# Forty-eight one-row reads from the Pool queue beside a saturated load stream

## The chip, the cores and the metric

The kernel runs on one core of one Trainium2 chip. The metric is device microseconds of one execution. The time before is the median of three runs.

## The reference

Two independent problems, A and B, have the same shapes, and their outputs stand side by side. Each is one step of decoding with attention over a window of a cache, for two batch entries, 32 query heads and 16 key/value heads of width 128. Cut to what matters:

```python
def ref(x, k_cache, v_cache, wq, wo):          # x [2, 1, 576], caches [2, 16, 16384, 128]
    W = 4096                                    # only the last 4096 positions are used
    q = (x @ wq).reshape(B, 1, 32, 128).transpose(0, 2, 1, 3)
    k = repeat(k_cache[:, :, Sk - W:, :], 2, axis=1)
    v = repeat(v_cache[:, :, Sk - W:, :], 2, axis=1)
    p = softmax(einsum("bhqd,bhkd->bhqk", q, k) * 128 ** -0.5)
    o = einsum("bhqk,bhkd->bhqd", p, v)
    return o.transpose(0, 2, 1, 3).reshape(B, 1, 4096) @ wo   # wo [4096, 576]
out = concatenate([ref(A), ref(B)], axis=-1)    # [2, 1, 1152], bfloat16
```

All tensors are bfloat16. The windows of the keys and values, with the two pairs of weights, make 153 MB that have to be read from HBM once.

## The kernel before

The work is cut into 16 slabs (`NSLAB`). A slab is one problem, one group of four key/value heads and one batch entry: its keys are one transfer of 4096 KB (called K), its values another (called V). Two slabs with the same heads and the two batch entries form a group G, and there are eight groups. A ring of four slots in SBUF (`ring`, `NSLOT = 4`) holds K and V transfers in turn.

All of these loads, and those of the weights `wq` and `wo`, are issued from SP's queue in one fixed order: K of slab t, then V of slab t - 3, with a `wo` piece (M or W) after every second group. SP issues a load when the slot's last reader is done: the second transpose of a K slab on DVE, or the last product with a V slab on PE.

One turn of the main loop (`for t in range(NSLAB)`, L664) does, for slab t: two transposes of K on DVE, one for each half (`make_X`, L433, into `xt`), each followed by the score products on PE (`make_S`, L459 and, through the helper, L264, into `st`); the products need a mask of queries, `zq`, which Pool builds two slabs ahead (`make_Z`, L425). For the group before, it takes the maximum on DVE (`make_max`, L467), reduces it on Pool (`mv` and `m`, L469 and L470), turns `m` on PE (L473), takes the negative maximum on DVE (`nM`, L480), repeats it on Pool (`nMrep`, L483), and forms the bias of the exponentials (L487 on PE, L490 on DVE, L497 on ACT). The probabilities are transposed on DVE (`pT`, L506), and the value products of slab t - 3 run on PE (L536), scaled and reduced on DVE (L559, L566).

Each engine runs its instructions in the order in which the program adds them; between engines there are semaphores. The order on Pool in an odd turn t is: `rsum` of a group, then `zq` of slab t + 2. In the even turn after it: `mv` and `m` of the group just finished, `zq`, `nMrep`. A `zq` waits until PE has finished the scores of slab t.

`sel` is a constant of 128 partitions by 4 x 128 elements, built on Pool at the start (L208). Four products on PE at the start (L307, `op_qs`) read it to spread the queries, and nothing reads it afterwards.

At the end of the program SP waits until both outputs have been written:

```python
        emit("sp", nc.sync)
        nc.sync.wait_ge(out_sem, dma_count[out_sem])
```

Before the change Pool issues no transfer. ACT's queue issues five small ones: four of two rows for `x` at the start and one output.

Of the kernel before, what the change touches and what calls it, by code (L numbers as in the profile page):

```python
# [62 lines left out]
def build_kernel(nc, probs, out):  # L63
# [4 lines left out]
    x0, k0, v0, wq0, wo0 = probs[0]  # L68
# [24 lines left out]
    with es:  # L93
# [15 lines left out]
        sel = sb("sel", [128, 4, 128], BF16)  # L109
# [44 lines left out]
        sem = lambda name: es.enter_context(nc.semaphore(name))  # L154
# [7 lines left out]
        wo_sem = [sem("wo%d" % r) for r in range(2)]  # L162
        x_sem = [sem("xload%d" % P) for P in range(NPROB)]
        out_sem = sem("outdone")

        S = _Sched()
        dma_count = {}

        def dma_op(eng, sem_h, n_dmas, fn, deps, tag):
            op = S.add(eng, fn, deps, tag)  # L170
            dma_count[sem_h] = dma_count.get(sem_h, 0) + 16 * n_dmas
            op.dma = (sem_h, dma_count[sem_h])
            return op
# [16 lines left out]
        pool = lambda fn, deps, tag: S.add("pool", fn, deps, tag)  # L190
# [61 lines left out]
        def tb_job(fn, tag, deps):  # L252
            n = tbn[0]
            tbn[0] += 1
            bank = TB
            d = list(deps)
            if n >= 1:
                d.append(tb_consumer[n - 1])
            op = pe(lambda e, bank=bank: fn(e, bank), d, tag)
            return n, bank, op  # L260
# [48 lines left out]
        n_, bank_s, op_qs = tb_job(f_qs, "qs", [qte, p_sel])  # L309
# [101 lines left out]
        def make_Z(t):  # L411
            P, g, b = t // (2 * GP), (t // 2) % GP, t % 2
            deps = [qs_ev, p_zq, d_bm]
            if t >= 2:
                deps.append(Sop[(t - 2, 1)])

            def f(e):
                for kp in range(2):
                    m = 2 * b + kp
                    b0 = zq[:, 0, m, 16 + 4 * m:16 + 4 * m + 1]  # L420
                    dst = bass.AP(b0.tensor, b0.offset, [list(b0.ap[0]), [4 * 144, 4], [32, 4], [1, 4]])
                    o = b * Hq + 8 * g + 4 * kp
                    src = qs[:, P, :].rearrange("d (p w) -> d p w", p=4)[:, :, o:o + 4].unsqueeze(2).broadcast_to([128, 4, 4, 4])
                    msk = bmask[:, 0:4].unsqueeze(1).unsqueeze(3).broadcast_to([128, 4, 4, 4])
                    last = e.tensor_tensor(dst, src, msk, ALU.mult)  # L425
                return last
            Zop[t] = pool(f, deps, "Z%d" % t)

        def make_X(t, jh):
            ensure(("K", t))  # L430
            r = slot_of[("K", t)]
            deps = [stream_dma[("K", t)][0][2], Sop[(t - 1, jh)] if t >= 1 else d_xT[1]]
            Xop[(t, jh)] = dve(lambda e: e.transpose(  # L433
                xt[:, jh, :].bitcast(FP32).rearrange("p (kp x kt) -> p x kp kt", kp=2, kt=2),
                ring[:, r, jh * HW_:(jh + 1) * HW_].bitcast(FP32).rearrange("p (x kp kt) -> p x kp kt", kp=2, kt=2)), deps, "X%d_%d" % (t, jh))
            if jh == 1:
                last_reader[("K", t)] = Xop[(t, jh)]

        def make_S(t, jh):
            G, b = t // 2, t % 2  # L440
            st = STT[G % 2]
            deps = [Xop[(t, jh)], Zop[t]]
            if b == 0 and G >= 2:
                deps.append(exp_op[G - 2])

            def f(e):
                for kp in range(2):
                    for p4 in range(4):
                        b32, par = p4 // 2, p4 % 2
                        m = 2 * b + kp  # L450
                        wt = zq[:, p4, m, 16 - 16 * jh:144 - 16 * jh]
                        first = b == 0 and jh == 0 and kp == 0 and p4 == 0
                        for bk in range(2):
                            o = 4096 * kp + 2048 * bk + 32 * b32 + par
                            b0 = xt[:, jh, o:o + 1]
                            mv_ = bass.AP(b0.tensor, b0.offset, [list(b0.ap[0]), [64, 32], [2, 16]])
                            ob = st[:, 512 * bk:512 * bk + 512]
                            if bk == 0:
                                last = e.matmul(ob, wt, mv_, start=first, stop=True, skip_group_check=True)  # L459
                            else:  # L460
                                last = mm_held(e, ob, wt, mv_, first)
                return last
            Sop[(t, jh)] = pe(f, deps, "S%d_%d" % (t, jh))

        def make_max(G):
            st = STT[G % 2]
            ch[(G, "max")] = dve(lambda e: e.tensor_reduce(mx[:], st[:, :].rearrange("p (x t) -> p t x", t=2), AX.X, ALU.max),  # L467
                                 [Sop[(2 * G + 1, 1)]] + prev(G, "pick"), "max%d" % G)
            ch[(G, "mult")] = pool(lambda e: e.tensor_tensor(mv[:], mx[:], v2[:], ALU.mult), [ch[(G, "max")], p_v2] + prev(G, "pick"), "mult%d" % G)  # L469
            ch[(G, "pick")] = pool(lambda e: e.tensor_tensor(m1[:], mv[:, 0:1], mv[:, 1:2], ALU.add), [ch[(G, "mult")]] + prev(G, "Tm"), "pick%d" % G)  # L470

        def make_Tm_pe(G):
            n, b, op = tb_job(lambda e, bank: e.transpose(bank[0:1, 0:128], m1[:, 0:1], ident_f[:]), "Tm%d" % G, [ch[(G, "pick")], p_ident_f])  # L473
            ch[(G, "Tm")] = op
            tm_job[G] = (n, b)
# [27 lines left out]
        def make_pT(G):  # L503
            v = G % 2
            deps = [exp_op[G]] + ([PVop[2 * (G - 2) + 1]] if G >= 2 else [qt_op])
            pT_op[G] = dve(lambda e: e.transpose(  # L506
                pT[:, v, :].rearrange("p (w j q) -> p j w q", w=4, q=8),
                pR[:].rearrange("p (j w q) -> p j w q", w=4, q=8)), deps, "pT%d" % G)

        def make_rsum(G):  # L510
            ch[(G, "rsum8")] = pool(lambda e: e.tensor_tensor(
                rsum8[:], rsum4[:, 0:4].unsqueeze(1).broadcast_to([128, 2, 4]), bsel[:, 0:2].unsqueeze(2).broadcast_to([128, 2, 4]), ALU.mult),
                [exp_op[G], d_bs] + prev(G, "sums"), "rsum8_%d" % G)
# [150 lines left out]
        for t in range(NSLAB):  # L664
            i = t - LAG
            odd = t % 2 == 1
            Gc = (t - 2) // 2 if not odd and t >= 2 else None
            Gs = (t - 3) // 2 if odd and t >= 3 else None
            Gd = (t - 5) // 2 if odd and t >= 5 else None
            Gp = (t - 6) // 2 if not odd and t >= 6 else None  # L670
            make_X(t, 0)
            make_S(t, 0)
            if i >= 1:
                make_evac(i - 1)
            if Gp is not None:
                make_pick(Gp)
            if Gc is not None:
                make_max(Gc)
            if Gs is not None:
                make_rsum(Gs)  # L680
                make_pT(Gs)
            if Gc is not None:
                make_Tm_pe(Gc)
            make_X(t, 1)
            make_S(t, 1)
            if t + 2 < NSLAB:
                make_Z(t + 2)
            if Gc is not None:
                make_nM(Gc)
            if Gs is not None:  # L690
                make_sums(Gs)
            if Gd is not None:
                make_dg(Gd)
            if Gp is not None and Gp % 2 == 1:
                make_projm(Gp // 2)
                if (Gp + 1) % GP == 0:
                    make_E(Gp // GP)
            if Gc is not None:
                make_bias(Gc)
            if t == T:  # L700
                make_max(NG - 1)
                make_pick(Gd)
            if i >= 0:
                make_PV(i)
# [34 lines left out]
        for e in ENGS:  # L739
            n = 0  # L740
# [13 lines left out]
        for op in order:  # L754
            have = seen[op.eng]
            need = {}
            for d in op.deps:
# [3 lines left out]
                k = id(s_h)  # L761
# [14 lines left out]
        def emit(eng_name, engine):  # L776
            for op in S.ops[eng_name]:
                for s_h, val in waits_of[id(op)]:
                    engine.wait_ge(s_h, val)
                last = op.fn(engine)  # L780
                if op.dma is None:
                    last.then_inc(ev[eng_name], 1)

        emit("sp", nc.sync)
        nc.sync.wait_ge(out_sem, dma_count[out_sem])
        emit("pe", nc.tensor)
        emit("dve", nc.vector)
        emit("act", nc.scalar)
# [35 lines left out]
```

## Time and profile before

| | before |
|---|---|
| median of 3 runs | 363.18 us (363.11 to 363.32) |
| profiled execution: span from first to last instruction | 361.8 us |
| mean granted TensorE clock | 0.849 |
| PE / DVE / ACT / POOL busy, share of the span | 66% / 60% / 13% / 7% |
| SP's queue (q1), share of 16 DMA engines' span | 98.7% |
| read from HBM | 153.10 MB, 423 GB/s over the span |

The profiled execution's time is known only as its span; the difference to the median, 1.4 us, is what lies around it. Matmuls are pipelined, so a busy PE is not PE at its peak. The share of the DMA engines is the mean over the core's 16. A packet is one piece of a transfer on one DMA engine; a completion is the packet of 4 bytes that counts up a semaphore when the pieces before it are written. In the views, a bracket behind a line gives the idle time before it and what ended it.

### The profile page before, as it was taken

To read this page: it belongs to the slowest core of one execution; us is meant where nothing else is said; L and a number is where in the kernel's file an instruction comes from. 1 tells how busy PE (TensorE), PEld (TensorE's weight loads), DVE (VectorE), ACT (ScalarE), POOL (GpSimd) and SP (SyncE) were. 2 spreads that over 40 slices of the span, in tenths; PEclk is the share of its full clock that TensorE was granted. 3 is DMA by queue.
4 is the path that set the end of the run, shared out by engine and by line. 5 is a ranking of instruction groups with operands and counts; after the bars stand their busy time and mean duration, and the time that the engine had idled before them with its cause. 6 is when DMAs were issued, how large, how long until landed. Compare 5 with 4: busy or idle time off the path is not lost.

```text
span 361.8 us, 2625 instructions
## 1 busy us (share of the span) xinstructions
PE 240.2 (66%) x1292; PEld 57.2 (16%) x927; DVE 218.7 (60%) x150; ACT 46.0 (13%) x78; POOL 24.3 (7%) x84
## 2 busy tenths in 40 slices
PE   0497787666485747662596675567776875668695
PEld 0000111112111201111121121112112121112222
DVE  1901898495929591934909585682927776674622
ACT  1002100040023000500005000500005000500500
POOL 4200101100010001000010000100010001000000
PEclk9999698969988996888788796888688796868969
DMA  8999999999999999999999999999999999999996
GB/s 327 457 435 406 460 408 446 424 431 438 417 453 408 457 404 428 444 431 431 435 420 444 417 449 410 440 431 438 424 442 412 449 417 429 435 435 431 417 412 256
DMA packets 6227, 153.26 MB, mean 424 GB/s; under 512 B 700, under 2 KB 840, under 8 KB 1224
## 3 DMA queue, kind: packets, MB, share of 16 engines
q1 hardware_dynamic: 6196, 153.10, 98.7%
q8 instruction: 8, 0.13, 0.1%
q14 instruction: 3, 0.02, 0.0%
q10 hardware_dynamic: 20, 0.01, 0.0%
HBM read 153.10 MB, written 0.00 MB: 423 GB/s over the span
## 4 chain that ended last, share of the span: by engine, by line
DMA 48%; DVE 26%; PE 16%; issue 8%; ACT 1%; POOL 0%; SPq 0%
DMA ring<-in_B_k_cache_dram 17%; DVE xt L433 16%; DMA ring<-in_A_k_cache_dram 13%; DMA ring<-in_B_v_cache_dram 9%; DMA ring<-in_B_wq_dram 7%; PE st L264 5%; PE st L459 5%; DMA wob<-in_B_wo_dram 3%; PE pj L264 2%; DVE oR L566 2%; DVE mx L467 2%; DVE pT L506 2%; DVE tmp L559 2%; PE ot L536 2%; PE pj L618 1%
## 5 line engine op out<-in xcount | busy, mean ns | idle before, releaser
L459 PE MATMUL st<-xt,zq 128*128 128x512 bf16 x256 | 124.1, 485 | 86.1 <-DVE xt L433 86.1
L433 DVE STREAM_TRANSPOSE xt<-ring 128x4096 f32<-128x4096 f32 x32 | 141.5, 4427 | 28.0 <-DMA ring<-in_A_k_cache_dram 18.8
L264 PE MATMUL st<-xt,zq 128*128 128x512 bf16 x256 | 122.7, 479 | 0.0
L497 ACT ACTIVATE pR<-st,bias 128x512 bf16<-128x512 f32 x32 | 40.0, 1414 | 222.9 <-DVE bias L490 222.9
L459 PEld LDWEIGHTS st<-xt,zq 128*128 128x128 bf16 x256 | 29.4, 115 | 210.1 <-issue 107.7
L536 PE MATMUL ot<-ring,pT 128*32 128x512 bf16 x512 | 32.6, 396 | 3.9 <-DMA ring<-in_B_v_cache_dram 3.9
L490 DVE SCALAR_TENSOR_TENSOR bias<-vmask,tb,offm 128x4 f32<-128x4 f32 x8 | 1.8, 223 | 43.0 <-PE tb L487 43.0
L520 DVE TENSOR_REDUCE ssum<-tb 128x2 f32<-128x8 f32 x8 | 1.3, 162 | 36.0 <-PE tb L517 36.0
L425 POOL TENSOR_TENSOR zq<-qs,bmask 128x64 bf16<-128x64 bf16 x32 | 8.7, 293 | 168.1 <-PE st L264 145.8
L506 DVE STREAM_TRANSPOSE pT<-pR 128x2048 bf16<-128x2048 bf16 x8 | 18.4, 2303 | 0.8 <-ACT pR L497 0.7
L279 PE MATMUL ot<-ring,pT 128*32 128x512 bf16 x18 | 7.6, 421 | 15.0 <-DMA ring<-in_A_wq_dram 14.2
L559 DVE SCALAR_TENSOR_TENSOR tmp<-ot,rsb,dmask 128x512 f32<-128x512 f32 x16 | 11.5, 719 | 7.9 <-PE ot L536 7.9
L566 DVE TENSOR_REDUCE oR<-tmp 128x128 f32<-128x512 f32 x15 | 15.6, 1042 | 0.5
L536 PEld LDWEIGHTS ot<-ring,pT 128*32 128x32 bf16 x512 | 12.4, 99 | 19.6 <-DMA ring<-in_B_v_cache_dram 5.5
L618 PE MATMUL pj<-wob,oM 128*2 128x288 bf16 x48 | 12.7, 299 | 0.0
L264 PE MATMUL pj<-wob,oM 128*2 128x288 bf16 x48 | 12.7, 299 | 0.0
L264 PE MATMUL pj<-ring,pT 128*32 128x512 bf16 x36 | 11.9, 416 | 0.0
L467 DVE TENSOR_REDUCE mx<-st 128x2 f32<-128x1024 f32 x8 | 9.7, 1213 | 0.1
L497 ACT ACTIVATION_READ_ACCUMULATOR pR<-st,bias 128x1 f32 x32 | 8.8, 276 | 0.0
L264 PE MATMUL st<-ring,pT 128*32 128x512 bf16 x18 | 7.3, 407 | 0.0
L222 DVE TENSOR_TENSOR xt<-xt,hmask 4x1152 bf16<-4x1152 bf16 x2 | 2.7, 1349 | 6.7 <-DMA xt<-in_A_x_dram 6.7
L469 POOL TENSOR_TENSOR mv<-mx,v 128x2 f32<-128x2 f32 x8 | 1.6, 195 | 75.8 <-DVE mx L467 75.8
(68 smaller groups left out, 75.6 us busy)
## 6 DMA issues: line engine op xcount, KB each, us to landing
ring<-in_A_k_cache_dram SPq DMA_DIRECT2D x8, 4096.0 KB, 24.3
ring<-in_A_v_cache_dram SPq DMA_DIRECT2D x8, 4096.0 KB, 29.9
ring<-in_B_k_cache_dram SPq DMA_DIRECT2D x8, 4096.0 KB, 27.0
ring<-in_B_v_cache_dram SPq DMA_DIRECT2D x7, 4096.0 KB, 29.8
ring<-in_A_wq_dram SPq DMA_DIRECT2D x1, 4608.0 KB, 13.3
ring<-in_B_wq_dram SPq DMA_DIRECT2D x1, 4608.0 KB, 23.8
wob<-in_A_wo_dram SPq DMA_DIRECT2D x2, 2304.0 KB, 28.3
wob<-in_B_wo_dram SPq DMA_DIRECT2D x1, 2304.0 KB, 27.4
```

What stands on the lines that cost most here:

```text
L264: return e.add_instruction(mybir.InstMatmult(name=nc.get_next_instruction_name(), engine=mybir.EngineType.PE, ins=[e.lower_ap(mv_), e.lowe ...
L279: last = e.matmul(QB[c], wt, mv_, start=first, stop=True, skip_group_check=True)
L425: last = e.tensor_tensor(dst, src, msk, ALU.mult)
L433: Xop[(t, jh)] = dve(lambda e: e.transpose(xt[:, jh, :].bitcast(FP32).rearrange("p (kp x kt) -> p x kp kt", kp=2, kt=2), ring[:, r, jh * H ...
L459: last = e.matmul(ob, wt, mv_, start=first, stop=True, skip_group_check=True)
L467: ch[(G, "max")] = dve(lambda e: e.tensor_reduce(mx[:], st[:, :].rearrange("p (x t) -> p t x", t=2), AX.X, ALU.max), [Sop[(2 * G + 1, 1)]] ...
L497: last = e.activation(pR[:].rearrange("p (x k) -> p k x", k=4)[:, kv, :], st[:, :].rearrange("p (x t) -> p t x", t=2)[:, kv % 2, :], ACTF.Exp,
L506: pT_op[G] = dve(lambda e: e.transpose(pT[:, v, :].rearrange("p (w j q) -> p j w q", w=4, q=8), pR[:].rearrange("p (j w q) -> p j w q", w= ...
L536: last = e.matmul(OTB[32 * c:32 * c + 32, :], pT[:, v, base + 32 * c:base + 32 * c + 32], ring[:, r, jj * 128:(jj + 4) * 128], start=rd == ...
L559: evac_op[i] = dve(lambda e: e.scalar_tensor_tensor(tv, o, rsb[:, v, b:b + 1], dm, ALU.mult, ALU.mult), deps, "ev%d" % i)
L566: ch[(G, "red%d" % b)] = dve(lambda e: e.tensor_reduce(oR[:, b, :], tmp[:].rearrange("p (j d) -> p d j", j=4), AX.X, ALU.add), [evac_op[i] ...
L618: last = e.matmul(PJ[h], oM[:, j, :], mv_, start=start and j == 0, stop=True, skip_group_check=True)
```

## The change

A function `make_rows(n, k0, k1)` issues transfers from Pool's queue, one for each k from k0 up to k1. Transfer k reads the first 18 + 2k elements (36 to 66 bytes) of row k of problem A's `wo` and writes them to partition k of `sel`, at element 64n. It is called in turns 3, 5, 7, 9, 11 and 13, after `zq` of slab t + 2 has been added: with k from 0 to 7 in turns 3, 7 and 11, and from 8 to 15 in turns 5, 9 and 13, and with n = 0, 1, 2. That makes 48 transfers, and each size occurs three times. All count on a new semaphore, `row_sem`. What they write is not read. SP waits for all of them at the end, behind its wait for the outputs.

```diff
+        row_sem = sem("rows")
...
+        def make_rows(n, k0, k1):
+            for k in range(k0, k1):
+                def f(e, k=k):
+                    return e.dma_start(sel[k:k + 1].rearrange("p a f -> p (a f)")[:, 64 * n:64 * n + 18 + 2 * k],
+                                       probs[0][4][k:k + 1, 0:18 + 2 * k]).then_inc(row_sem, 16)
+                dma_op("pool", row_sem, 1, f, [op_qs], "rows%d_%d" % (n, k))
...
             if t + 2 < NSLAB:
                 make_Z(t + 2)
+            if t in (3, 5, 7, 9, 11, 13):
+                make_rows((t - 3) // 4, 8 * ((t - 3) // 2 % 2), 8 * ((t - 3) // 2 % 2) + 8)
...
         nc.sync.wait_ge(out_sem, dma_count[out_sem])
+        nc.sync.wait_ge(row_sem, dma_count[row_sem])
```

## The prediction

> **What bounds the kernel now.** I read the busy table by slices first, then the same stream by stages, then the waits and the time line of the Pool engine, and last the end of the chain. The slices show which resource is never idle:
>
> ```profile
> DMA  8999999999999999999999999999999999999996
> GB/s 327 457 435 406 460 408 446 424 431 438 417 453 408 457 404 428 444 431 431 435 420 444 417 449 410 440 431 438 424 442 412 449 417 429 435 435 431 417 412 256
> DMA packets 6227, 153.26 MB, mean 424 GB/s; under 512 B 700, under 2 KB 840, under 8 KB 1224
> q1 hardware_dynamic: 6196, 153.10, 98.7%
> ```
>
> Every slice but the first and the last has the 16 DMA engines nine tenths busy or more, and one queue, SP's q1, holds 98.7% of 16 engines' span: 0.987 x 361.8 = 357 us of packets. No compute engine passes 66%. By stages (columns: PE, PEld, DVE, ACT, POOL busy, granted clock, DMA share, GB/s):
>
> ```profile
> 0.00:1.80 1.80, 0.00 (x0) 0.00 (x0) 0.14 (x1) 0.00 (x0) 1.06 (x8) 1.00 0.00 1
> 25.00:350.00 325.00, 222.30 (x1179) 53.68 (x848) 205.63 (x125) 44.14 (x76) 17.53 (x64) 0.83 1.00 430
> 359.20:361.80 2.60, 0.65 (x8) 0.26 (x8) 0.45 (x1) 0.40 (x1) 0.00 (x0) 1.00 0.00 1
> ```
>
> From 25 to 350 us the share is 1.00 at 430 GB/s. There is no gap into which another packet could fall: whatever a packet takes on a DMA engine is added to what comes after it on that engine, and the last weights land that much later. The 1.8 us ahead of the stream and the 2.6 us behind it stay. The end hangs on that landing:
>
> ```profile
> 350.11 9.14 DMA wob<-in_B_wo_dram
> 359.25 0.04 issue
> 359.30 0.70 PE pj L639 x8
> 360.00 0.02 issue
> 360.02 0.45 DVE out_sb L655
> ```
>
> The profiled execution spans 361.8 us; the median of the runs is 363.18, so 1.4 us lie around the span. I carry them over and add my sum to 363.18. A measurement can tell about 0.2%, 0.73 us, from no change.
>
> **The change part by part.** Nothing is removed and nothing is moved. Added are 48 transfers of 36 to 66 bytes, eight behind the zq of each of slabs 3, 5, 7, 9, 11 and 13, and one wait of SP at the very end. The rows land in `sel`, whose only readers are the four products of L307, done by 37.2 us; nobody waits for a row but SP's last wait.
>
> *Pool's time.* Each transfer is issued by Pool, in order, so it stands ahead of the max of the next group (mv, L469) and of nMrep (L483). The room for it is the idle time ahead of mv in those slabs:
>
> ```profile
> 87.17 0.55 POOL L425 TENSOR_TENSOR zq<-qs,bmask 128x64 bf16<-128x64 bf16 x2 [10.46 <-PE st L264]
> 94.89 0.19 POOL L469 TENSOR_TENSOR mv<-mx,v 128x2 f32<-128x2 f32 x1 [7.17 <-DVE mx L467]
> 132.16 0.20 POOL L469 TENSOR_TENSOR mv<-mx,v 128x2 f32<-128x2 f32 x1 [8.48 <-DVE mx L467]
> 217.61 0.19 POOL L469 TENSOR_TENSOR mv<-mx,v 128x2 f32<-128x2 f32 x1 [8.24 <-DVE mx L467]
> ```
>
> The six gaps are 7.2, 8.5, 13.5, 8.2, 11.3 and 8.2 us. The page has no issue from Pool. Its nearest rows are SP's and ACT's: SP takes 0.32 us for the output row and 0.54 for a slab, ACT 0.81 for two. Eight of 0.54 are 4.3 us and fit everywhere. The longest instruction that Pool ran, 1.42 us (L245), is my upper end: eight are 11.4 us, over the smallest gap by 4.2. That delay has two covers. Behind mv come the turn of m on PE (L473) and nM on DVE, and DVE first spends 4.43 us in the transpose of the slab's second half (94.72 to 99.15 in slab 4) while PE waits 3.15 us for it; about 3.5 us are hidden there. What remains would make DVE late with the next transposes, and so SP late with the next slab, but SP issues far ahead. A slab of 4096 KB takes 9.7 us at 430 GB/s and lands 24 to 30 us after its issue; in the packet records the shortest time from a slab's issue to its first packet, once the ring is full, is 9.0 us (issue at 83.12, first packet at 92.13). So Pool's time costs 0 in the sum, and costs nothing until one issue takes about (7.2 + 3.5 + 9.0) / 8 = 2.5 us.
>
> *The DMA engines' time.* This is the whole price. Its count: either all 16 engines are visited by each transfer, or a transfer of one row goes to one engine. The ACT queue's rows bear on this: five transfers of two rows left 20 packets on q10, ten of 1152 B and ten of 4 B, so two engines each, a data packet and a completion. By that row a single row visits one engine. If it is the same engine each time, that engine gets 48 visits and sets the end; if all 16 are visited, every engine gets 48; only if the one engine rotates are there three visits to each. I take 48 visits on the engine that decides, and keep three as the low end.
>
> Its price per visit: the 690 completions of 4 B on q1 took 9 ns each and stood back to back with their neighbours, which overlap by 3 ns: 6 ns net. A packet of 1152 B took 51 ns and one of 4096 B 159, so a line through both puts 66 B at 11 ns. The output row of the first problem, sent from ACT in mid-stream at 277.95 us, held its engine for 59 ns, data and completion, and the stream's next packet took 1213 ns, as usual. So a visit costs from 6 ns (a completion alone) to 59 ns. I take 20 ns, 11 for the data and 9 for the completion, as the payload is near the 4-byte end. 48 x 0.020 = 0.96 us. The ends are 3 x 0.006 = 0.02 us and 48 x 0.059 = 2.8 us.
>
> The Trainium skill speaks to the count, in "DMA: Bandwidth & Descriptors", in the section on why a DMA increments its semaphore by 16: a transfer issued from GpSimd makes all 16 engines post the completion, whatever its shape, where one from SP or ACT uses only the engines that carry data. The ACT rows show the second half; no row here shows the first. By that rule alone the completions would make 48 x 9 ns = 0.43 us on every engine.
>
> *SP's last wait.* The wait for the output (L785) is an instruction of 17 ns. The second stands behind it, and its 48 increments are there since some 300 us: +0.02 us.
>
> Sum: 0 + 0.96 + 0.02 = +1.0 us, **364.2 us**.
>
> **The rivals.**
>
> *Not slower (same).* The visits rotate over the engines, or a visit costs only its 6 ns. The place is q1's stream on the slowest engine, the price 0.02 to 48 x 0.009 = 0.43 us, so 363.2 to 363.6; it decides as long as a visit stays under 0.73 / 48 = 15 ns. For it: 9 ns per completion is the best supported price on the page, and in the records no stall follows one. Against it: rows and completions of a second queue come on top of that.
>
> *An entrance fee.* Packets that come from a queue other than SP's and ACT's may stall an engine. The nearest rows are the instruction loads (q8, q14). The eight of 16 KB took 1.03 to 1.11 us each, and the stream's next packet ran 0.47 to 0.55 us over its normal time: 1.57 us together, where a 16 KB packet of q1 took 0.61. The three of 8 KB in the stream came to 0.69, 0.96 and 0.99 by the same sum. Twice the 8 KB figure less the 16 KB one leaves a fee at zero bytes of -0.19 to +0.42 us, 0.19 in the mean. Paid once per batch of eight, at its upper end, 6 x 0.42 = +2.5 us, 365.7; paid at each visit in the mean, 48 x 0.19 = +9 us, 372. For it: these are the only rows with a queue not written by SP or ACT. Against it: most of the excess grows with the size, as if the target were slow, and the second queue that is like q1 shows none.
>
> *Pool becomes the bound.* Above 2.5 us an issue the covers are gone; at 3 us, a batch takes 24, which is 4 us over the 19.7 of slab 3, and up to 4 us in the batches with gaps near 8: about +4 to +15 us, 367 to 378. For it: nothing on the page is an issue from Pool. Against it: no Pool instruction here is over 1.42 us. The skill's page "SBUF — State Buffer" warns of this in its box on the trap that "DVE blocks DMA": GpSimd cannot write descriptors while DVE holds the port that they share, in its two-port modes, and it gives 3.1 us for a transfer of 0.62 beside such a copy. This trace speaks against it for this DVE work: zq took 292 to 296 ns in all 32 cases, with transposes beside many of them. By that figure eight issues would make 25 us, and this rival would hold.
>
> *Faster.* A gain would need fewer bytes or a shorter head or tail. The change touches none; only a lucky skew of the 16 engines' ends (358.9 to 359.2 us) is left, 0.3 us at most.
>
> **How the numbers follow.** The sum's own case, 0.73 to 2.8 us slower, has 0.45. The same-time rival has 0.30: it rests on the same rows with the smaller price. The entrance fee has 0.15, Pool as the bound 0.06, a gain 0.04. Slower by over 0.2% is 0.45 + 0.15 + 0.06 = 0.66, within it 0.30, faster 0.04. The likeliest case's own range is 363.9 to 366.0. For eight in ten I go down to 363.4, inside the same-time case, which leaves out about 0.12, and up to 369, which takes in the fee per batch and leaves out about 0.08.
>
> **What would show it.** In the changed profile: a new queue in the list with small packets, their number telling the count (96 or so if one engine carries a row, over 768 if all 16 post); a DMA share that stays 1.00 from 25 to 350 us while the last weights land about 1 us later than 359.2; a tail of 2.6 us as before; the mv of slabs 4, 6 and 10 later by less than 4.4 us, and no new wait of DVE for a K slab. I am wrong if the stream has gaps (Pool or SP late), if the stream's packets beside the new ones grow from 1.21 us, or if the landing does not move.

## The result and the profile after

The changed kernel takes 363.79 us (median of 18 runs, 363.69 to 364.56) against 363.18 (18 runs). The ratio is 1.0017, with an interval of 1.001 to 1.0024: 0.6 us slower, between 0.4 and 0.9. That is inside the predicted range of 363.4 to 369 and 0.4 us under the predicted 364.2; at 0.17% it lies just under the 0.2% that the prediction took as its bound, so in the case that it gave 0.30.

The page of the changed kernel, the load of the DMA engines and the list of queues:

```profile
DMA  8999999999999999999999999999999999999996
DMA packets 7763, 153.27 MB, mean 423 GB/s; under 512 B 2236, under 2 KB 2376, under 8 KB 2760
q1 hardware_dynamic: 6196, 153.10, 98.5%
q0 software_dynamic: 1536, 0.01, 0.2%
```

The stream is the same 6196 packets and 153.10 MB. The new queue, q0, has 1536 packets for 48 transfers: 32 for each, whatever its length. In the packet records 768 of them are completions of 4 B; the rest carry the row in pieces of 4, 6, 8, 34, 38 or 46 B, or fill up to 16 with 4 B. The records don't name the engine, but where the engines are full each packet starts 3 to 5 ns before the end of the one ahead of it, so the 16 sequences can be followed: about 96 of the new packets lie on each. So each transfer puts two packets on every one of the 16 engines. Their mean time is 9.05 ns. (A row is 18 to 48 elements of 2 bytes, so 36 to 96 bytes; the 66 given above as the longest is the mean.)

The groups and the time line of Pool in slab 3 (start, duration, line, what; in brackets the idle time before):

```profile
L469 POOL DMA_DIRECT2D sel<-in_A_wo_dram x48 | 24.8, 523 | 0.0
...
87.31 0.55 POOL L426 TENSOR_TENSOR zq<-qs,bmask 128x64 bf16<-128x64 bf16 x2 [10.46 <-PE st L265]
87.80 4.37 POOL L469 DMA_DIRECT2D sel<-in_A_wo_dram  x8
95.03 0.19 POOL L477 TENSOR_TENSOR mv<-mx,v 128x2 f32<-128x2 f32 x1 [2.86 <-DVE mx L475]
```

One issue takes 0.52 us of Pool, a batch of eight 4.1 to 4.4 us, and in slab 3 the last 2.86 us of the gap ahead of mv stay idle. mv waits for the maximum on DVE as before, in all six slabs.

The stages and the end of the chain:

```profile
25.00:350.00 325.00, 219.00 (x1186) 53.16 (x856) 205.59 (x125) 44.34 (x76) 42.01 (x112) 0.86 1.00 429
359.90:362.50 2.60, 0.65 (x8) 0.26 (x8) 0.45 (x1) 0.40 (x1) 0.00 (x0) 1.00 0.00 1
...
348.28 11.74 DMA wob<-in_B_wo_dram
360.02 0.04 issue
360.07 0.70 PE pj L647 x8
```

The share stays 1.00, the last weights land 0.8 us later than in the trace before (360.02 against 359.25), and the tail behind them has the same 2.6 us. The packet records show where the time came in. For each load of the stream I take the end of its 16 completions, in the mean over the engines, against the same load before the change. Ahead of the first row this trace is already 0.14 us late, the same for the loads near 44, 73 and 83 us: a difference between two executions. Less that, the load near 131 us is 0.12 us late, the one near 205 us 0.31, near 288 us 0.54, near 342 us 0.64, and the last weights 0.60. The delay grows with the batches, is not in one place, and stops growing once the last row is in (312 us).

### The profile page after: what moved, and what is told of

Read it like the earlier page. It is cut to its first block, busy times and chain, and to the rows that moved or that the text cites. A ratio compares the mean times of both kernels' runs of the same rounds, so it can differ in the third digit from the quotient of the medians.

```text
span 362.5 us, 2674 instructions
## 1 busy us (share of the span) xinstructions
PE 236.3 (65%) x1293; PEld 56.6 (16%) x927; DVE 218.6 (60%) x150; ACT 46.0 (13%) x78; POOL 48.8 (13%) x132
## 3 DMA queue, kind: packets, MB, share of 16 engines
q1 hardware_dynamic: 6196, 153.10, 98.5%
q0 software_dynamic: 1536, 0.01, 0.2%
HBM read 153.10 MB, written 0.00 MB: 422 GB/s over the span
## 4 chain that ended last, share of the span: by engine, by line
DMA 42%; DVE 29%; PE 18%; issue 8%; ACT 1%; POOL 1%; SPq 0%
DVE xt L434 18%; DMA ring<-in_B_k_cache_dram 17%; DMA ring<-in_B_v_cache_dram 9%; DMA ring<-in_B_wq_dram 7%; PE st L265 6%; PE st L460 6%; DMA ring<-in_A_k_cache_dram 6%; DMA wob<-in_B_wo_dram 3%; DVE oR L574 3%; DVE pT L514 2%; PE pj L265 2%; DVE mx L475 2%; DVE tmp L567 2%; ACT pR L505 1%; PE pj L626 1%
## 5 line engine op out<-in xcount | busy, mean ns | idle before, releaser
L460 PE MATMUL st<-xt,zq 128*128 128x512 bf16 x256 | 122.2, 477 | 88.5 <-DVE xt L434 88.5
L265 PE MATMUL st<-xt,zq 128*128 128x512 bf16 x256 | 121.1, 473 | 0.0
L544 PE MATMUL ot<-ring,pT 128*32 128x512 bf16 x512 | 31.6, 386 | 7.5 <-DMA ring<-in_B_v_cache_dram 7.5
L469 POOL DMA_DIRECT2D sel<-in_A_wo_dram x48 | 24.8, 523 | 0.0
L280 PE MATMUL ot<-ring,pT 128*32 128x512 bf16 x18 | 7.6, 421 | 15.3 <-DMA ring<-in_A_wq_dram 14.5
L519 POOL TENSOR_TENSOR rsum<-rsum,bsel 128x8 f32<-128x8 f32 x8 | 1.6, 204 | 56.5 <-ACT pR L505 56.5
```

The lines of the kernel that those rows point to most:

```text
L265: return e.add_instruction(mybir.InstMatmult(name=nc.get_next_instruction_name(), engine=mybir.EngineType.PE, ins=[e.lower_ap(mv_), e.lowe ...
L469: return e.dma_start(sel[k:k + 1].rearrange("p a f -> p (a f)")[:, 64 * n:64 * n + 18 + 2 * k], probs[0][4][k:k + 1, 0:18 + 2 * k]).then_i ...
L544: last = e.matmul(OTB[32 * c:32 * c + 32, :], pT[:, v, base + 32 * c:base + 32 * c + 32], ring[:, r, jj * 128:(jj + 4) * 128], start=rd == ...
```

## The experiments

Theory A: a Pool transfer costs the stream two small packets on each engine, 9 ns each less the 3 ns or so by which neighbours overlap, 12 ns in all; 48 x 12 = 0.58 us. Rivals: B, a fee per batch, or for having the queue and the last wait; C, Pool's time on the path. Each run was timed beside the kernel before on the same chip (363.20 to 363.22 us there).

**The changed kernel again.** 

> The changed kernel again, beside these. All theories: 363.8 us, +0.6 us over before; it gives the yardstick on this chip.

Measured: 363.81 us against 363.22, ratio 1.0016 (1.0007 to 1.0025).

**Pool busy for as long, without transfers.** The batch is replaced by eight memsets, and `row_sem` and its wait are gone:

```diff
-                dma_op("pool", row_sem, 1, f, [op_qs], "rows%d_%d" % (n, k))
+            for _ in range(8):
+                busy.append(pool(lambda e: e.memset(sel[:].rearrange("p a f -> p (a f)"), 0.0), [busy[-1]], "busy%d" % len(busy)))
```

> No transfer at all: in place of each batch Pool runs eight memsets of sel, about 0.55 us each, so about 4.4 us as the eight issues took, and there is neither a Pool queue nor SP's last wait. Theory A: no packet, so 0 (363.2 us). Rival C (Pool's time): +0.6 us as the change. Rival B (the queue or the wait): 0.

Measured: 363.20 us, ratio 1.0 (0.9991 to 1.0008). Pool's time is not the cause; C falls for batches of this length.

**Six transfers in place of 48.** One transfer of eight rows by 34 elements per batch, at the same places, with the wait:

```diff
-            for k in range(k0, k1):
...
+                return e.dma_start(sel[k0:k1].rearrange("p a f -> p (a f)")[:, 64 * n:64 * n + 34],
+                                   probs[0][4][k0:k1, 0:34]).then_inc(row_sem, 16)
```

> One transfer of eight rows of 34 elements per batch in place of eight transfers of one row: 6 transfers from Pool at the same six places, with the queue and SP's last wait kept. Theory A: the transfers count, not the rows: if each again puts two packets on every engine, 12 x 6 ns = 0.07 us, with the wait +0.1 us. Rival B (a fee per batch, or for the queue and the wait): +0.6 us as the change.

Measured: 363.20 us, ratio 1.0 (0.9991 to 1.0008). Its page, the line of the new queue:

```profile
q0 software_dynamic: 192, 0.00, 0.0%
```

192 packets for six transfers are again 32 each, while eight rows travel in one. The queue, the semaphore, the wait and the six places are all there, and the time is that of the kernel before: B falls. What counts is the number of transfers.

**Twice as many.** The eight reads of a batch are issued again into other partitions of `sel`:

```diff
+            for c in range(2):
                 for k in range(k0, k1):
-                    return e.dma_start(sel[k:k + 1]...
+                    return e.dma_start(sel[16 * c + k:16 * c + k + 1]...
```

> The same reads issued twice: 96 transfers, sixteen behind the zq of each of the six slabs; the copies go to other partitions of sel. The trace of the changed kernel shows 1536 packets on Pool's queue for 48 transfers, 32 each, so two on each of 16 engines, at 9 ns less 3 ns of overlap. Theory A (packets on a full stream): 96 x 2 x 6 ns = 1.15 us, with SP's wait +1.2 us over before. Rival B (a fee per batch, or for the presence of Pool's queue and the last wait): the batches are still six, so +0.6 us as with 48. Rival C (Pool's time delays the chain behind mv): eight issues of 0.51 us left mv where it was; sixteen take 8.2 us and pass the gaps of 7.2 to 8.5 us only just, so it can't tell more than a few tenths.

Measured: 364.80 us, ratio 1.0043 (1.003 to 1.0056): +1.6 us, between 1.1 and 2.0. A's 1.2 lies inside the interval, and the median is 0.4 above it. The queue:

```profile
q0 software_dynamic: 3072, 0.01, 0.5%
```

The stream's own packets held an engine for 357.12 us before, 357.20 with 48 transfers and 357.35 with 96; but a second trace of the changed kernel has 357.28, so that a stretch of these packets adds to A is not shown.

**126 transfers.** 21 per batch. 

> 21 reads per batch, 126 in all, the first sixteen rows repeated into other partitions of sel. Theory A: 126 x 12 ns = 1.5 us, by the growth that 96 showed (1.6 us, 16.6 ns each) up to 2.1: +1.5 to +2.1 us. Pool's 10.8 us per batch is under the 41.5 - 27.3 = 14.2 us that two slabs leave. With 192 transfers Pool halted ahead of the 129th for 41 us, until all 128 before it had landed; if that goes by the count, 126 show no halt.

Measured: 364.94 us, ratio 1.0048 (1.0034 to 1.0062): +1.7 us, or 13.8 ns per transfer. The sixth batch left without a halt:

```profile
294.33 10.58 POOL L469 DMA_DIRECT2D sel<-in_A_wo_dram  x21
```

The landings of the stream, taken as above (mean of the engines, less what was there before the first row), measure the price more finely than the run times. The load near 342 us is 0.64 us late with 48 transfers, in both traces of the changed kernel, and 1.31 with 96; with 126, whose last row is in at 350 us, the loads behind that are 1.75 late. That is 13 to 14 ns per transfer, whatever the count; the six transfers gave 0.06 us and the eight memsets -0.02. A has 12; where the other 1 to 2 ns are is not shown.

**Long rows.** 512 elements of each row instead of 18 to 48:

```diff
-                    return e.dma_start(sel[k:k + 1].rearrange("p a f -> p (a f)")[:, 64 * n:64 * n + 18 + 2 * k],
-                                       probs[0][4][k:k + 1, 0:18 + 2 * k]).then_inc(row_sem, 16)
+                    return e.dma_start(sel[16 * n + k:16 * n + k + 1].rearrange("p a f -> p (a f)"),
+                                       probs[0][4][k:k + 1, 0:512]).then_inc(row_sem, 16)
```

> 48 reads from Pool as in the change, but of 512 elements (1024 bytes) each. Theory A: the count of packets stays 1536, the data packets are of 64 bytes, whose service on the line through the 1152-byte and 4096-byte packets is 11 ns in place of 9: 48 x (6 + 8) ns = 0.67 us, +0.7 us. Rival (the payload sets the price): 18 times the mean bytes, 49 KB in all, 3 KB on each engine, 0.1 us at 27 GB/s, on top of whatever the change costs: +0.7 us as well; a much larger time would say that short rows are not what is cheap.

Measured: 363.88 us, ratio 1.0018 (1.0009 to 1.0027). Its queue:

```profile
q0 software_dynamic: 1536, 0.05, 0.3%
```

The same 1536 packets, now 64 B and 4 B, at a mean of 10.0 ns. The landings are 0.71 us late where the short rows had 0.64. With some 15 times the bytes the price is nearly the same.

**One engine alone.** Reads of 17 elements from ACT's queue:

```diff
-                    return e.dma_start(sel[k:k + 1].rearrange("p a f -> p (a f)")[:, 64 * n:64 * n + 18 + 2 * k],
-                                       probs[0][4][k:k + 1, 0:18 + 2 * k]).then_inc(row_sem, 16)
-                dma_op("pool", row_sem, 1, f, [op_qs], "rows%d_%d" % (n, k))
+                    return e.dma_start(sel[k:k + 1].rearrange("p a f -> p (a f)")[:, 64 * n:64 * n + 17],
+                                       probs[0][4][k:k + 1, 0:17]).then_inc(row_sem, 16)
+                dma_op("act", row_sem, 1, f, [op_qs], "rows%d_%d" % (n, k))
```

> 48 reads of 17 elements (34 bytes, a count that doesn't divide) from ACT's queue instead of Pool's, at the same places. A transfer of one piece has one data packet and one completion, and if ACT's queue puts them on the same engine each time, that engine gets 96 packets as in the change, while all 16 together get 96 and not 1536. Theory A in the form that the slowest engine sets the end: 96 x 6 ns = +0.6 us, as the change. Rival: the end goes by the mean over the engines: 0.6 / 16 = +0.04 us, or the engines' ends have slack. The trace shows which engine carries what only by the count of packets.

Measured: 363.30 us, ratio 1.0001 (0.9992 to 1.001). The page has 96 packets more on ACT's queue (20 before):

```profile
q10 hardware_dynamic: 116, 0.01, 0.0%
```

In the records they follow one another every 1.22 us within a batch, data and completion in turn, as on one engine. That it is the same engine in every batch the records don't say, but the steady lead in the next run fits it; it then carries as many packets as each of the 16 does in the change. The 0.6 us that the first form of the theory expected didn't come.

**One engine, twice as many.** 96 such reads. 

> The reads of 17 elements from ACT's queue, twice as many: 96 transfers, sixteen at each of the six places. With 48 the trace showed data packet and completion of one transfer after another, 1.22 us apart, as on one engine, and the time rose by 0.09 us and not 0.6. Theory: the slowest engine sets the end, and the loaded engine had a lead: in the kernel before, the last 16 completions of the stream lie 0.6 us apart. Now 192 packets x 6 ns = 1.15 us on that engine, less a lead of 0.3 to 0.6 us: +0.5 to +0.9 us. Rival: the end goes by the mean over the engines, 1.15 / 16 = 0.07, so +0.1 to +0.2 us.

Measured: 363.32 us, ratio 1.0005 (0.9996 to 1.0014). The time went the rival's way, but the records show why it isn't a mean over the engines. The engine that carries the reads can be told in them: where a small pair is 12 ns apart, a completion of the stream stands between. At 82.83 us it finished its part of a slab 1.08 us ahead of the slowest engine; by 308.74 us the lead was down to 0.54. It shrank by 0.05 to 0.06 us with every slab during the batches (0.97, 0.91, 0.85 us in three that follow each other), in which it had eight small packets per slab: 7 ns each. It grew only where the slowest engine was held up itself (0.98 to 1.22 in the load that landed near 113 us, 1.05 to 1.37 near 148). So each packet did cost its 6 to 7 ns, and the engine paid from a lead. The lead never ran out, so what comes then was not run. In the run with 48 reads the lead was 1.4 to 1.9 us. The 0.6 us that I had taken for the lead was a misreading: the last 16 completions in order of time belong to several transfers. By the updates of the last weights' semaphore the 16 engines of the kernel before end 2.0 us apart (357.62 to 359.62 us).

**Four times as many.** 32 reads per batch, 192 in all. 

> The same reads issued four times: 192 transfers, 32 behind the zq of each of the six slabs. Theory A: 192 x 2 x 6 ns = 2.3 us, +2.3 us over before. Rival B (fee per batch): +0.6 us. Rival C: a batch holds Pool for 32 x 0.51 = 16.5 us, 8 to 9 us past the gaps ahead of mv; if that were on the path, the six batches would cost up to about 40 us; by the covers of the prediction (3.5 us of DVE transpose and at least 9 us of issued loads) it costs nothing beyond A.

Measured: 411.77 us, ratio 1.1321 (1.1304 to 1.1338): +48.6 us. None of the three theories had this. The time line of Pool at the fifth batch:

```profile
258.32 0.54 POOL L426 TENSOR_TENSOR zq<-qs,bmask 128x64 bf16<-128x64 bf16 x2 [11.35 <-PE st L265]
300.21 15.93 POOL L470 DMA_DIRECT2D sel<-in_A_wo_dram  x32 [41.35 <-issue]
```

Four batches, 128 transfers, have left. The fifth stands still for 41.35 us, with no wait of the program ahead of it. By the packet records 81 of the 128 were done when it should have left, the last at 291.69 us, and the 129th left 8.5 us after that. The semaphore's own updates come later: the last of the 128 counted at 298.40 us, 1.81 us ahead of the 129th. The stages before and during the halt:

```profile
217.00:259.00 42.00, 26.02 (x136) 6.11 (x102) 25.94 (x17) 5.00 (x8) 17.98 (x40) 0.80 1.01 427
259.00:300.00 41.00, 6.09 (x50) 1.53 (x40) 12.47 (x7) 0.00 (x0) 0.00 (x0) 0.63 0.76 317
300.00:345.00 45.00, 22.24 (x114) 5.21 (x75) 13.43 (x8) 5.41 (x9) 17.59 (x38) 0.69 0.33 129
```

Up to 259 us the share is 1.01 although each batch held Pool for 16 us; then the stream runs dry.

**132 transfers.** 22 per batch. 

> 22 reads per batch, 132 in all. If Pool halts ahead of the 129th until the 128 before have landed, the halt falls into the sixth batch, near 295 us: by then some 92 have landed (0.45 per us since 88), the other 36 need up to 80 us at the stream's pace and less when the stream runs dry; with 192 the halt was 41 us, so +20 to +40 us. If the halt was a matter of the backlog or of the 16-us batches and not of the count, 132 x 12 to 17 ns: +1.6 to +2.2 us, as with 126.

Measured: 394.67 us, ratio 1.0855 (1.0832 to 1.0877): +31.5 us, where 126 cost 1.7. The sixth batch of this run, on Pool:

```profile
292.77 9.02 POOL L469 DMA_DIRECT2D sel<-in_A_wo_dram  x18
340.38 1.98 POOL L469 DMA_DIRECT2D sel<-in_A_wo_dram  x4 [38.59 <-issue]
```

Five batches of 22 and 18 more make 128; the 129th waits 38.59 us. 100 of the 128 were done when it should have left, the last at 335.77 us, 4.6 us ahead of its start. By the semaphore the last of them counted at 338.57 us, 1.81 us ahead, as with 192. So the halt goes by the count. That the last update is what ends it is the likely reading, with the same 1.81 us in both runs; what in Pool counts to 128 these runs don't show.

**Pool busy for 30 and for 18 us.** 52 and 31 memsets per batch, no transfer. 

> No transfer: Pool runs 52 memsets of sel per batch, about 28 us, in the six slabs. The prediction put the limit of its covers at 7.2 + 3.5 + 9.0 = 19.7 us for the tightest batch, 3.5 more or so elsewhere. By these covers the first batch alone loses 28 - 19.7 = 8 us and the six together +10 to +40 us; the DMA share falls below 1.00 behind the batches. If Pool's time never matters, 363.2 us; if there is no cover at all beyond the gaps ahead of mv, six batches lose 28 less 7 to 13 us each, about +110 us.

Measured: 459.52 us, ratio 1.2657 (1.2636 to 1.2677): +96.3 us, more than twice the upper end that the covers allowed. Its Pool:

```profile
87.95 30.19 POOL L469 MEMSET sel<- 128x512 bf16 x52
118.11 0.19 POOL L475 TENSOR_TENSOR mv<-mx,v 128x2 f32<-128x2 f32 x1
118.38 0.19 POOL L476 TENSOR_TENSOR m<-mv 128x1 f32<-128x1 f32 x1
124.33 0.54 POOL L425 TENSOR_TENSOR zq<-qs,bmask 128x64 bf16<-128x64 bf16 x2 [5.76 <-PE st L264]
...
144.24 0.54 POOL L425 TENSOR_TENSOR zq<-qs,bmask 128x64 bf16<-128x64 bf16 x2 [12.89 <-PE st L264]
144.72 5.76 POOL L469 MEMSET sel<- 128x512 bf16 x10
```

(The view ends at 150 us; the second batch takes 30.19 us as well.) From batch to batch it is 57 to 59 us: 30.2 of Pool, then mv, the turn of m, the scores, the next zq, two transposes and scores again, 27 us in which Pool does nothing long. The loads of two slabs and their share of `wo` take 41.5 us at 430 GB/s. So each batch loses 57.5 - 41.5 = 16 us, and six lose 96. This sum was made after the result and takes no lead off, so that it meets the 96.3 is no proof; the next run was its test.

> No transfer: 31 memsets per batch, 18.0 us at the 0.58 us each that they took with 52. The covers of the prediction (7.2 + 3.5 + 9.0 = 19.7 us) say no loss: 363.2 us. The other reading, from the run with 30.2 us per batch: two slabs took 57.5 us there, Pool's 30.2 and a chain of 27.3 that can't run beside it, where the stream needs 41.5 for two slabs; the lead of the issued loads is spent once and not made good. Then two slabs take 18.0 + 27.3 = 45.3 us, 3.8 more than the stream, six times 23 us, less a lead of at most 17: +6 to +23 us.

Measured: 384.91 us, ratio 1.0591 (1.0568 to 1.0614): +21.7 us, where the chain of 27.3 us gave 23 less a lead, and the covers gave 0. By the completions the loads were not late up to 205 us, with the third batch over, then 5 us late by 230 and 14 by 322, so a lead was spent first; the last 6 us came at the end of the stream, behind the batches, and the sum doesn't have them. Its waits for Pool's m (total, times, longest); before the change the first of them had 4.6 us in five:

```profile
PEld tb L479 <- POOL m L476: 58.2, 6, 11.0
PE tb L479 <- POOL m L476: 53.5, 6, 10.2
```

## Why the prediction was right or wrong, step by step

*The bound.* Right. The stream has no gap and every packet added on all engines comes out at the end; head and tail stayed.

*Pool's time.* The term of 0 was right, and the issue (0.52 us) was the 0.54 of SP's rows that it was measured with. The limit that went with it was wrong: 2.5 us per issue, from adding a gap, a transpose and the lead of the issued loads. The lead is spent once and not renewed for the next batch. By the chain that can't run beside Pool, two slabs leave it 41.5 - 27.3 = 14.2 us per batch, 1.8 us per issue: an estimate, between 10.8 us per batch, which cost nothing beside the packets (126 transfers), and 18 us, which cost 21.7.

*The count of visits.* 48 on every engine came out, but my reason for it was half wrong. I took the row of ACT's queue, one engine for one row, and held that a single engine loaded 48 times would set the end too. The two runs with one engine refute that: it had a lead of a microsecond and more. The count came out because Pool's transfers visit all 16 engines, so as far as my reason goes it was luck. Here the skill's rule was the better guide: "DMA: Bandwidth & Descriptors", in its section on why a DMA increments its semaphore by 16, says that all 16 engines post the completion, and the trace agrees, with 768 completions for 48 transfers. That rule is about completions alone; the trace has 16 more packets per transfer beside them, the row's pieces and those that fill up to 16.

*The price of a visit.* This is the mis-sized term: 20 ns taken, 12 by A and 13 to 14 measured by the landings (in the run times 0.6 us for 48, 1.6 for 96, 1.7 for 126, so 12 to 17). I had added service times, 11 + 9 ns, although the same paragraph had found that a packet overlaps its neighbours and adds 6 net. Two packets at 6 ns give 0.58 us, with SP's wait 0.6: the measured time. The rows' length was wrong too, 96 bytes at most and not 66, but on the line that was used this makes 12 ns of 11. The ends of the range, 6 and 59 ns, held it. By its own words the sum's case, slower by 0.73 us or more, did not come: the mark of 364.2 was 0.4 us high, and the measured 0.6 lies in the case that had 0.30, where the sum's own had 0.45.

*SP's wait.* +0.02 us was too small to be seen; the tail has the same 2.6 us.

*The rivals.* The same-time rival named a price of 0.02 to 0.43 us and a limit of 15 ns per visit; the price was 12 to 14 ns, so its condition held, and the measured 0.6 lies between its price and the sum's case. The entrance fee did not come: six transfers at the same six places cost nothing that shows (0.06 us in the landings). The rival of a gain took the engines' ends to lie 0.3 us apart; they lie 2.0 us apart, but nothing in the change used that. The skill's warning in "SBUF — State Buffer", in the box on DVE blocking a DMA from GpSimd, was not seen here: an issue took 0.50 to 0.78 us (median 0.51), and the first packet of a batch followed its first issue by 3.7 to 3.9 us in the five batches with a transpose on DVE beside it and by 3.8 us in the one without.

## What to carry to other kernels

Where a load stream fills the DMA engines, a small transfer costs the packets that it puts on each engine, net of the overlap, and not its bytes: from Pool that was 32 packets per transfer and 13 to 14 ns of the end, so rows belong in one transfer of several rows, which cost nothing measurable here. Load on one engine alone did not show in the time as long as that engine had a lead over the slowest one. Before calling time on a side engine hidden, add it to the chain that can't run beside it and compare the sum with the bound's time for the same work: a lead of issued loads covers one delay, not one per turn.

## What the runs showed that I had not expected

- Pool's 129th transfer left only after all 128 before it had landed, 1.81 us after the last update of their semaphore, with 132 and with 192 in the program: a halt of 39 and 41 us. With 126 there was none.
- A small transfer beside the stream lands late. The rows of the changed kernel landed 6.5 to 19.5 us after their issue, the later ones of a batch last: each of the two packets on an engine waited for one packet of 32 KB (1.22 us), so a batch of eight drains in some 20 us. Nobody waits for them here.
- The 16 engines of the kernel before run some 2.1 us apart in mid-stream (first to last completion of one slab), and 2.0 us at the end.
